# The first weight block on ScalarE's queue, and the first weight sums behind a product's outputs on VectorE

## The chip, the cores and the metric

The kernel runs on one core of a Trainium2 chip. The metric is the device time of one execution in microseconds (us), given as the median of several executions. "Span" is the time from the first to the last instruction of a profiled or recorded execution; it is some 1.8 us shorter than the time. Engines: PE is TensorE's matmul, PEld its weight load, DVE VectorE, ACT ScalarE, POOL GpSimd, SP SyncE. A name like L392 is line 392 of the kernel that ran; from the loads on, lines of the changed kernel are up to three lower than those of the kernel before.

## The reference, cut to what matters

```python
x = A_x
h = x + _A_ref(_layernorm(x), A_wqkv, A_wo)                      # local attention, 32 heads
h2 = h + _B_ref(_layernorm(h), B_w_gate, B_w_up, B_w_down)       # (gate * up) @ down
# x: 2048 x 1024 bf16; wqkv: 1024 x 3072; w_gate, w_up: 1024 x 3584; w_down: 3584 x 1024
```

The 2048 rows are processed in four chunks of 512. The last two chunks share their feed-forward stage, in 14 "pairs" of weight columns that use a Strassen-like scheme with seven products in place of eight; it needs sums of weight blocks (tile sw) and sums of activation blocks (tile prodx).

## The kernel before

Two places matter. The first is the head: the first row tiles, the first weight block, and the LayerNorm that the first matmuls wait for.

```python
    def load_x0(t):                        # one row tile, 128 x 1024: 262 KB
        nc.sync.dma_start(x0[t][:], x[bass.ds(t * 128, 128), :])
    def load_w0(lo, n):                    # half of the first weight block: 524 KB
        nc.sync.dma_start(w0[:, lo:lo + n, :], wqkv_v[:, lo:lo + n, 0:512])
    load_x0(0); load_x0(1); load_w0(0, 4); load_x0(2); load_w0(4, 4); load_x0(3)   # six lines in the kernel
    nc.scalar.preload_act_table_set("natural_log_exp_and_others")
    # ...
    first_half(0, 0); first_half(0, 1); first_rstd(0)   # statistics of row tile 0
    for t in range(4):
        if t < 3:
            first_half(t + 1, 0)           # half the statistics of the next tile, ahead of
        first_norm(t)                      # the normalization of this one
        # ... matmuls of tile t - 1 (first_mm), transposes of tile t on PE
```

The second is the joint between the down projection of chunk 1 and the first pair. `dprod` is 14 matmuls into an accumulator, `result` reads the accumulator on VectorE and stores rows.

```python
    def weight_sums(n, eng=nc.gpsimd):
        # ...
        if n == 0:
            nc.scalar.activation(wt[:], raw[:], ACTF.Copy, scale=scale_gu.s)   # tile ws, one op of 3.7 us
        # ...  four tensor_tensor on eng into sw
    # ...
    for t in range(4):
        ln_rows(3, t, l3)                  # ScalarE normalizes, then a DMA transposes into l3
    sub([dn["kx"], dn["vx"]], dn["21"], dn["11"])
    weight_sums(0, nc.vector)
    retire(2)
    # ...
    for q in range(2):
        dprod(ex[q], q, EF["21"], fcells(dn["12"]), False)
        nc.vector.tensor_tensor(et[:], p5t[:, q, :], hs1[2 + q][:, 512:1024], ALU.add)
        result(1, hs1[2 + q], 2 + q, 1, ex[q], dn["inv"], et)
    retire(1)
    activation_sums(l2, l3, dn["px"])      # four tensor_tensor on VectorE, read l2 and l3
    for q in range(2):
        dprod(ey[q], q, EF["12"], fcells(dn["22"]), False)
        nc.vector.tensor_tensor(p5t[:, q, :], p5t[:, q, :], hs1[q][:, 512:1024], ALU.add)
        result(1, hs1[q], q, 1, ey[q], dn["inv"], p5t[:, q, :])
    for q in range(2):
        dprod(ex[q], q, EF["22"], fcells([dn["kx"], dn["vx"]]), False)   # ex again
        result(1, hs1[2 + q], 2 + q, 0, ex[q], dn["inv"], None)
    # ... then pair 0, 1, ... 13
```

Of the kernel before, what the change touches and what calls it, by code (L numbers as in the profile page):

```python
# [78 lines left out]
def kernel(  # L79
# [11 lines left out]
    nc = tc.nc  # L91
# [18 lines left out]
    wqkv_v = A_wqkv.rearrange("(ko p) n -> p ko n", p=128)  # L110
# [62 lines left out]
    def retire(n=1):  # L173
        state["live"] -= n
        pump()
# [91 lines left out]
    w0 = wpool.tile([128, KO, 512], BF, tag="w", name="w_qkv_0")  # L267
# [4 lines left out]
    def load_x0(t):  # L272
        nc.sync.dma_start(x0[t][:], x[bass.ds(t * 128, 128), :])

    def load_w0(lo, n):
        nc.sync.dma_start(w0[:, lo:lo + n, :], wqkv_v[:, lo:lo + n, 0:512])

    load_x0(0)
    load_x0(1)
    load_w0(0, 4)  # L280
    load_x0(2)
    load_w0(4, 4)
    load_x0(3)
    nc.scalar.preload_act_table_set("natural_log_exp_and_others")
    warm = t1k.tile([128, TC], BF, tag="t1k", name="warm")
    nc.vector.memset(warm[:], 0.0)
# [363 lines left out]
    def weight_sums(n, eng=nc.gpsimd):  # L650
        raw = pair["w", n]
        wt = wpool.tile([128, KO, 2, 256], F16, tag="w", name=f"ws_{n}")
        if n == 0:
            nc.scalar.activation(wt[:], raw[:], ACTF.Copy, scale=scale_gu.s)
        else:
            nc.vector.tensor_scalar(wt[:], raw[:], scale_gu.s, None, ALU.mult)
        sw = wpool.tile([128, 2, 4, 4, 128], F16, tag="w", name=f"sw_{n}")
        for i in ((slice(0, 2),) if eng is nc.vector else (slice(0, 1), slice(1, 2))):
            a11, a21, a12, a22 = (wt[:, k:k + 4, i, c:c + 128].rearrange("p k i c -> p i k c")
                                  for k in (0, 4) for c in (0, 128))  # L660
            eng.tensor_tensor(sw[:, i, 0], a21, a22, ALU.add)  # L661
            eng.tensor_tensor(sw[:, i, 1], sw[:, i, 0], a11, ALU.subtract)
            eng.tensor_tensor(sw[:, i, 2], a11, a21, ALU.subtract)
            eng.tensor_tensor(sw[:, i, 3], a12, sw[:, i, 1], ALU.subtract)
        pair["a", n], pair["s", n] = wt, sw
        state["live"] += 1

    def activation_sums(l2, l3, room):
        b11, b12, b21, b22 = l2[:, 0:4, :], l3[:, 0:4, :], l2[:, 4:8, :], l3[:, 4:8, :]

        t1, t2, t3, t4 = (room[:, bass.ts(i, 4), :].bitcast(F16) for i in range(4))
        nc.vector.tensor_tensor(t1, b12, b11, ALU.subtract)
        nc.vector.tensor_tensor(t2, b22, t1, ALU.subtract)
        nc.vector.tensor_tensor(t3, b22, b12, ALU.subtract)
        nc.vector.tensor_tensor(t4, b21, t2, ALU.subtract)
        pair["b"] = (b11, b21, t1, t2, t3, t4, b22)
# [101 lines left out]
    def sub(dst, x0, x1, eng=nc.vector):  # L778
        for d, a0, a1 in zip(dst, x0, x1):
            eng.tensor_tensor(f16(d[:, 0:NH, :]), f16(a0[:, 0:NH, :]), f16(a1[:, 0:NH, :]), ALU.subtract)  # L780

    def fcells(homes):
        return [f16(t[:, k, :]) for t in homes for k in range(NH)]

    def dprod(ps, q, lhs, rhs, fresh, lo=0, n=TC):
        for k in range(NP):
            nc.tensor.matmul(ps[:, bass.ds(lo, n)], lhsT=lhs[k][:, bass.ts(q, 128)], rhs=rhs[k][:, bass.ds(lo, n)],  # L787
                             start=(fresh and k == 0), stop=(k == NP - 1), skip_group_check=not fresh)

    def result(c, rows, t, hf, ps, sc, other, lo=0, n=TC):  # L790
        cols = bass.ds(hf * 512 + lo, n)
        nc.vector.scalar_tensor_tensor(rows[:, cols], ps[:, bass.ds(lo, n)], sc,
                                       rows[:, cols] if other is None else other[:, bass.ds(lo, n)], ALU.mult, ALU.add)
        nc.sync.dma_start(outf[bass.ds(c * TC + t * 128, 128), cols], rows[:, cols])
# [175 lines left out]
    for t in range(4):  # L970
        ln_rows(3, t, l3)
    sub([dn["kx"], dn["vx"]], dn["21"], dn["11"])
    weight_sums(0, nc.vector)
    retire(2)
    et = att.tile([128, TC], F32, tag="t3", name="et")
    for q in range(2):
# [2 lines left out]
        result(1, hs1[2 + q], 2 + q, 1, ex[q], dn["inv"], et)  # L979
    retire(1)  # L980
    activation_sums(l2, l3, dn["px"])
    for q in range(2):
        dprod(ey[q], q, EF["12"], fcells(dn["22"]), False)
        nc.vector.tensor_tensor(p5t[:, q, :], p5t[:, q, :], hs1[q][:, 512:1024], ALU.add)
        result(1, hs1[q], q, 1, ey[q], dn["inv"], p5t[:, q, :])
# [140 lines left out]
```

## Time and profile before

| | kernel before |
|---|---|
| median time, 3 runs | 783.46 us (782.1 to 784.1) |
| the profiled execution | 781.72 us, span 779.9 us |
| PE busy | 766.8 us, 98% of the span |
| mean granted PE clock, profiled execution | 0.999 |
| largest wait of PE | 3.18 us, for the read of ex |

### The profile page before, as it was taken

The numbers are of one execution on the slowest core, as the hardware profiler recorded it, in microseconds if no ns is written. First come the engines' busy times: TensorE is split into PE (matmuls) and PEld (weight loads), VectorE is DVE, ScalarE is ACT, GpSimd is POOL, SyncE is SP. The second block draws the span as 40 slices with busy tenths as digits, with TensorE's granted clock in tenths as the row PEclk, the third lists the DMA queues.
The fourth block names the chain that finished last, engine by engine and source line by source line (L and its number), as shares of the span: only waits on it lengthen the run. The fifth ranks groups of instructions, "written<-read, shape, count | busy, mean of one in ns | idle before, by whom it ended". The sixth has DMA issues, their size and how long they took to land.

```text
span 779.9 us, 10436 instructions
## 1 busy us (share of the span) xinstructions
PE 766.8 (98%) x3648; PEld 355.0 (46%) x3707; DVE 614.9 (79%) x805; ACT 473.5 (61%) x1028; POOL 142.4 (18%) x152
## 2 busy tenths in 40 slices
PE   8999999999999999999999999989999999999997
PEld 6544444444444444444444444434444444444444
DVE  6629999999899998999979989975553444579862
ACT  5627445313576652966769799836677677788240
POOL 0000000010000200002000001008778677600000
PEclk9999999999999999999999999999999999999999
DMA  8999693896955868858555492824332323730001
GB/s 272 260 236 209 169 274 90 262 274 173 341 174 186 297 215 234 270 189 270 195 163 195 133 313 75 183 74 110 106 99 64 108 67 97 255 123 28 1 27 55
DMA packets 181605, 133.86 MB, mean 172 GB/s; under 512 B 79024, under 2 KB 174384, under 8 KB 179504
## 3 DMA queue, kind: packets, MB, share of 16 engines
q1 hardware_dynamic: 177968, 111.17, 50.1%
q0 software_dynamic: 3584, 22.02, 8.1%
q8 instruction: 29, 0.48, 0.3%
q14 instruction: 24, 0.20, 0.1%
HBM read 104.86 MB, written 22.02 MB: 163 GB/s over the span
## 4 chain that ended last, share of the span: by engine, by line
PE 88%; DVE 9%; ACT 1%; issue 1%; DMA 1%; SPq 0%; DVEq 0%
PE ps L392 20%; PE pu L392 12%; PE pg L392 12%; PE dx L787 6%; PE pz L680 6%; PE acc L626 6%; PE py L680 6%; PE px L680 6%; PE wo L513 4%; PE pv L680 3%; PE dy L787 3%; DVE h L834 1%; PE ps L355 1%; PE ex L787 1%; DVE prodx L780 1%
## 5 line engine op out<-in xcount | busy, mean ns | idle before, releaser
L392 PE MATMUL ps<-lnT,w_qkv 128*128 128x512 bf16 x721 | 158.9, 379 | 0.8
L392 PEld LDWEIGHTS <-w_qkv 128*128 128x128 bf16 x736 | 71.9, 98 | 85.9
L392 PE MATMUL pu<-lnT,w_wu 128*128 128x512 bf16 x438 | 105.1, 379 | 0.6
L392 PE MATMUL pg<-lnT,w_wg 128*128 128x512 bf16 x440 | 105.1, 379 | 0.4
L306 ACT CAST sg<-ps 128x512 bf16<-128x512 f32 x96 | 54.8, 590 | 54.4 <-PE ps L392 51.1
L475 DVE TENSOR_TENSOR pv<-vD,at 128x4096 bf16<-128x4096 bf16 x32 | 72.5, 2287 | 0.3
L432 DVE TENSOR_TENSOR prod<-qD,kD 128x4096 bf16<-128x4096 bf16 x32 | 72.3, 2284 | 0.1
L680 PEld LDWEIGHTS <-sw 128*128 128x128 f16 x448 | 43.8, 98 | 53.2 <-issue 0.4
L392 PEld LDWEIGHTS <-w_wg 128*128 128x128 bf16 x448 | 43.8, 98 | 52.9
L392 PEld LDWEIGHTS <-w_wu 128*128 128x128 bf16 x448 | 43.8, 98 | 52.9
L596 ACT CAST us<-pu 128x512 bf16<-128x512 f32 x56 | 33.2, 593 | 41.1 <-PE pu L392 38.7
L680 PE MATMUL px<-lnT,ws 128*128 128x512 bf16 x212 | 53.1, 379 | 0.6
L680 PEld LDWEIGHTS <-ws 128*128 128x128 f16 x336 | 32.9, 98 | 39.6
L626 PE MATMUL acc<-w_wd,gs 128*128 128x512 bf16 x219 | 48.2, 379 | 0.3
L487 POOL DMA_DIRECT2D od<-oD x4 | 2.2, 544 | 252.3 <-DVE oD L485 162.5
L661 POOL TENSOR_TENSOR sw<-ws 128x512 f16<-128x512 f16 x26 | 30.0, 1154 | 87.6 <-PE py L680 80.4
L591 ACT CAST gs<-pg 128x512 bf16<-128x512 f32 x56 | 32.9, 587 | 11.4 <-PE pg L392 9.3
L185 ACT ACTIVATE rs<-mv,eps 128x1 f32<-128x1 f32 (+1 forms) x25 | 7.4, 297 | 50.3 <-DVE mv L182 47.1
L434 DVE TENSOR_TENSOR prod<-prod 128x4096 bf16<-128x4096 bf16 x16 | 36.6, 2288 | 0.3
L541 ACT ACTIVATE junkd<-w_wd 128x512 bf16<-128x512 bf16 x56 | 34.3, 613 | 0.0
L626 PEld LDWEIGHTS <-gs 128*128 128x128 bf16 x224 | 21.9, 98 | 26.4
L697 ACT COPY py<-px 128x512 f32<-128x512 f32 x28 | 16.0, 570 | 29.6 <-PE px L680 29.6
(304 smaller groups left out, 1398.0 us busy)
## 6 DMA issues: line engine op xcount, KB each, us to landing
w_wg<-in_B_w_gate_dram SPq DMA_DIRECT2D x14, 1024.0 KB, 6.6
w_wu<-in_B_w_up_dram SPq DMA_DIRECT2D x14, 1024.0 KB, 5.3
w_wd<-in_B_w_down_dram SPq DMA_DIRECT2D x8, 896.0 KB, 7.4
w_pair<-in_B_w_gate_dram SPq DMA_DIRECT2D x14, 512.0 KB, 4.0
w_pair<-in_B_w_up_dram SPq DMA_DIRECT2D x14, 512.0 KB, 5.2
w_wo<-in_A_wo_dram SPq DMA_DIRECT2D x6, 1024.0 KB, 8.4
w_qkv<-in_A_wqkv_dram SPq DMA_DIRECT2D x5, 1024.0 KB, 9.1
kd<-sg SPq DMA_DIRECT2D x32, 144.0 KB, 2.9
```

The costliest lines, as they stand in the source:

```text
L306: nc.scalar.copy(sg[:, HB:HB + TC], ps[:])
L392: nc.tensor.matmul(ps[:], lhsT=wt[:, ko, bass.ts(j, 128)], rhs=rhs[:, ko, :], start=(ko == 0), stop=(ko == KO - 1))
L432: nc.vector.tensor_tensor(prod[:, j], qD[:], kD[:, :, o:o + SUB], ALU.mult)
L434: nc.vector.tensor_tensor(prod[:, :, 0:16], prod[:, :, 0:16], prod[:, :, 16:32], ALU.add)
L475: nc.vector.tensor_tensor(pv[:, j], vD[:, :, o:o + SUB], at[:, w, None, :].to_broadcast((128, DH, SUB)), ALU.mult)
L513: nc.tensor.matmul(ps[:], lhsT=oTs[c][:, kk, t, :], rhs=wts["wo", c, hf][:, kk, :], start=(kk == 0), stop=(kk == KO - 1))
L541: nc.scalar.activation(junk, src, ACTF.Abs, accum_out=self.l1[:, k:k + 1])
L591: nc.scalar.copy(gs[:], pg[:])
L596: nc.scalar.copy(us[:], pu[:])
L626: nc.tensor.matmul(acc[t][:], lhsT=hT[f][:, bass.ts(t, 128)], rhs=wts["wd", c, hf, b][:, j, :], start=(f == 0), stop=(f == NF - 1))
L680: nc.tensor.matmul(ps[:], lhsT=lhs[:, ko, :], rhs=rhs[:, ko, :], start=(fresh and ko == 0), stop=(ko == 3), skip_group_check=not fresh)
L787: nc.tensor.matmul(ps[:, bass.ds(lo, n)], lhsT=lhs[k][:, bass.ts(q, 128)], rhs=rhs[k][:, bass.ds(lo, n)], start=(fresh and k == 0), stop=( ...
```

## The change

The intent of its first part (A) is that the weights don't queue between the row tiles: ScalarE issues the two weight halves while SyncE issues the rows. The intent of its second part (B) is that VectorE reads the accumulators of a finished product before it waits for ScalarE's conversion and makes weight sums, so that PE can go on.

```diff
     def load_w0(lo, n):
-        nc.sync.dma_start(w0[:, lo:lo + n, :], wqkv_v[:, lo:lo + n, 0:512])
-
-    load_x0(0)
-    load_x0(1)
+        nc.scalar.dma_start(w0[:, lo:lo + n, :], wqkv_v[:, lo:lo + n, 0:512])
+
     load_w0(0, 4)
-    load_x0(2)
     load_w0(4, 4)
-    load_x0(3)
+    for t in range(4):
+        load_x0(t)
     nc.scalar.preload_act_table_set("natural_log_exp_and_others")
@@
     sub([dn["kx"], dn["vx"]], dn["21"], dn["11"])
-    weight_sums(0, nc.vector)
     retire(2)
@@
     activation_sums(l2, l3, dn["px"])
+    weight_sums(0, nc.vector)
     for q in range(2):
```

## The prediction

> **What bounds the kernel now.** I read the page first. TensorE (PE) is busy for nearly the whole span, and the table of waits of PE alone then shows what is left of its idle time:
>
> ```profile
> span 779.9 us, 10436 instructions
> PE 766.8 (98%) x3648; PEld 355.0 (46%) x3707; DVE 614.9 (79%) x805; ACT 473.5 (61%) x1028; POOL 142.4 (18%) x152
> ```
>
> ```profile
> PE ex L787 <- DVE h L792: 3.2, 1, 3.2
> PE warm_ps L300 <- DVE warm L286: 1.2, 1, 1.2
> ...
> PE ps L355 <- DMA w_qkv<-in_A_wqkv_dram: 0.2, 1, 0.2
> PE pv L680 <- DVE h L792: 0.2, 1, 0.2
> ```
>
> The columns are waiter, what it waited for, us in total, count, longest. The largest single wait is one of 3.2 us by a matmul into the accumulator ex, for VectorE's line 792, which reads the finished sums out of ex. The diff touches exactly this place, and the place of the 0.2 us wait for w_qkv. The timeline around the first (start, duration, engine, instruction, idle time before it) gives the order:
>
> ```profile
> 503.96 2.02 DVE L780 TENSOR_TENSOR vx<-w_dn,w_dn 128x3584 f16<-128x3584 f16 x1
> ...
> 506.69 3.69 ACT L654 ACTIVATE ws<-w_pair,sbgu 128x4096 f16<-128x4096 bf16 x1
> ...
> 510.42 0.69 DVE L661 TENSOR_TENSOR sw<-ws 128x1024 f16<-128x1024 f16 x1 [4.44 <-ACT ws L654]
> ...
> 513.75 0.75 DVE L792 SCALAR_TENSOR_TENSOR h<-ex,inv_h1d,et 128x512 bf16<-128x512 f32 x1
> ...
> 514.56 1.67 PE L787 MATMUL ex<-kx,gs 128*128 128x512 f16 x7 [3.18 <-DVE h L792]
> ...
> 516.00 1.22 DVE L672 TENSOR_TENSOR prodx<-lnT,lnT 128x2048 f16<-128x2048 bf16 x1
> ...
> 520.67 0.68 DVE L984 TENSOR_TENSOR ep<-ep,h 128x512 f32<-128x512 f32 x1
> ...
> 524.37 1.02 PE L680 MATMUL pv<-prodx,sw 128*128 128x512 f16 x4 [0.16 <-DVE h L792]
> ```
>
> VectorE stands still for 4.44 us for ScalarE's conversion ws, then makes the weight sums sw, and only then reads ex, which PE had finished at about 505.2. Behind it come the four activation sums (L672 to L675) and four results. From 460 to 524 the chain that ended last runs mostly over VectorE; from 524 to the last stage it runs over PE without a gap. So time taken from this spot should come off the end one for one.
>
> Last, the start of the timeline:
>
> ```profile
> 3.54 1.29 DVE L330 BATCH_NORM_STATS2 st<-x 128x6 f32<-128x512 bf16 x2 [2.38 <-DMA x<-in_A_x_dram]
> ...
> 5.67 0.73 DVE L342 TENSOR_SCALAR ln<-x,mv,rs 128x512 bf16<-128x512 bf16 x2
> ...
> 8.50 0.62 PE L355 MATMUL ps<-lnT,w_qkv 128*128 128x128 bf16 x8 [0.24 <-DMA w_qkv<-in_A_wqkv_dram]
> 8.76 0.69 DVE L330 BATCH_NORM_STATS2 st<-x 128x6 f32<-128x512 bf16 x1
> ```
>
> The first row tile is there at 3.54 and starts the LayerNorm; the second half of the first weight block is there at 8.5, and PE lost only 0.24 us on it.
>
> [...]an issue takes 0.40 to 0.51 us on SyncE, while between 4 and 8 us the DMA engines are fully busy (shares 1.08, 1.02, 0.99, 1.05 in the windows of 1 us). [...]The activation sums took 1216 to 1226 ns, [...]and moving them doesn't change their cost. [...]L792 ran at 513.75, though its input had long been ready.
>
> **Part B, the weight sums behind the results.** No instruction is added or removed; the order on VectorE changes. ScalarE has no work between ws and the copies of the pair, so ws still runs at 506.69 to 510.4.
> - Two adds and two results (L978, L792) took from 512.96 to about 516.0, that is 3.0 us. They can follow vx, which ends at 505.98, so they end at about 509. PE finishes its product into ey at about 511.4 and goes on to ex at once: the 3.18 us wait is gone.
> - The activation sums need the last transposed LayerNorm rows. The last of the eight transposes (L870) was issued at 507.7, and these take 3.2 to 3.3 us to land: about 511.0. The DMA engines agree: share 1.09 at 509 to 510, 0.26 at 510 to 511, 0 after. VectorE thus still waits, about 2 us, now for a DMA: from 509 to 511.05.
> - Then four activation sums, 516.00 to 520.67 before: 4.67 us, to 515.7. Then four weight sums, 510.42 to 512.96 before: 2.54 us, to 518.3. ws is long ready.
> - L984 and the results thus start at 518.3 instead of 520.67: 2.4 us earlier. PE ends ex at 511.4 + 6.04 (28 matmuls) = 517.4 and the two px products at 519.15. Then its first pv needs the bank of ey: it was read at 522.2 before, now at 519.8 (PE waits 0.65 us). The second pv needs that of ex: 524.37 before, now about 521.95 (PE waits about 0.4 us).
> So part B gives **2.4 us**, not 3.2: VectorE's chain is the bound in the end, and its new start is the landing of the transposes. GpSimd's sums for pair 1 and later loads move along.
>
> **Part A, the first loads.** It removes nothing from the 2.10 MB to be loaded: four row tiles of 262 KB, two half weight blocks of 524 KB. Rates in the windows from 1 us on: 27, 289, 275, 366, 357, 313, 385, 86 GB/s. Added up (316 KB at 3 us, 591 at 4, 957 at 5, 1314 at 6, 1627 at 7, 2012 at 8), in the order of before the bytes of row tile 0 are through at 2.8, tile 1 at 3.8, weight half 1 at 5.3, tile 2 at 6.0, weight half 2 at 7.5. Tile 0 is used at 3.54 and weight half 2 at 8.5, so the landing adds some 0.75 to 0.95 us. SyncE issues tile 0 at 0.76 already; ScalarE's two issues take an estimated 0.9 us ahead of its table load of 1.28 us, which ends at about 3, before its first work at 5.10: harmless. What changes is who shares the DMA engines:
> - **Equal bytes for both queues:** tile 0 is through when 524 KB are, at 3.8, so used at about 4.5; tile 1 at 5.3, used at 6.05, and VectorE reads half of it before it normalizes tile 0. Normalization moves from 5.67 to about 6.7; weight half 2 comes last, at about 9. The second tile's transposes start at about 9.7 instead of 8.9: **+0.8 us**.
> [...]
> - **A rate without the dips** (370 GB/s from 1.9 us on): all landed at 8.4, tile 0 at 4.1: **+0.35 us**.
> From 8.5 on PE is busy without a break, so a later start moves everything. I take **+0.55 us**.
>
> **Sum:** 783.46 - 2.4 + 0.55 = 781.6.
>
> **Rivals.** (1) *The head gets faster*: if the rows keep their time and both weight halves come earlier, the 0.24 us wait goes and the head gains 0.2: 780.9. For it: the issues of all rows end at 2.6 instead of 3.7. Against: the DMA engines are full from 4 to 8 us. (2) *The new wait eats part B*: if the transposes land later, or the weight sums turn out to hold PE at the first pv for longer, B gives 1 us or less: 783. For it: eight transposes queued for 13.4 us. Against: the DMA engines run dry at 510.3. (3) *The whole 3.3 us come off* (both waits of PE): 780.7. Against: VectorE's chain counted above. (4) *The head suffers more*, over 1.5 us, if weights go ahead of rows: 782.6.
>
> **Range and chances.** All these lie between 780.7 and 783. The three timed runs of before spread from 782.1 to 784.1, so a median may be off by some 0.8 us. That makes 779.9 to 783.3. 2% are 15.7 us; no rival comes near, so same 0.98, and 0.01 on each side.
>
> **What would show it.** Right: no 3.2 us wait of PE for L792; VectorE waiting about 2 us for the transposes ahead of L672; weight sums directly behind L675; two waits of PE of half a us ahead of pv; first normalization later than 5.67, at 6 to 6.7. Wrong: L672 starting well before or after 511; normalization at 5.67 or earlier; a second 3 us wait in the pair stage; or the last stage, from the pairs' end to the end of the span, taking other than its 89.6 us.

The sum is 783.46 - 2.4 + 0.55 = 781.6. Its 0.55 us for part A was my choice among cases of how two queues share the DMA engines, and one of them (+0.6 us) is cut: it took over a rule of sharing that no run here shows. The two that stand, +0.8 and +0.35 us, rest on an assumption, equal bytes for both queues; only their rates and landing times are worked out from the profile of the kernel before.

## The result, and the profile after

| | before | after |
|---|---|---|
| median time, 4 runs each | 783.59 us (782.1 to 784.1) | 780.18 us (779.73 to 780.64) |
| span of the profiled execution | 779.9 us | 778.0 us |
| PE busy in it | 98% | 99% |

The ratio is 0.996, 95% interval 0.9942 to 0.9977. Ratios here are the mean time of one kernel's fast runs over that of the other's of the same rounds, so not quite the ratio of the medians. The verdict at 2% is "same", the time is inside the predicted range. But the medians differ by 3.4 us, and the two profiled executions by 2.0 us (781.72 and 779.73). The prediction of 1.85 us matches the profiles, not the medians.

The waits of PE in the changed kernel (waiter, waited for, us in total, count, longest):

```profile
PE warm_ps L298 <- DVE warm L284: 1.2, 1, 1.2
PE pv L678 <- DVE h L790: 0.9, 2, 0.7
...
PE ps L353 <- ACT lnT L348: 0.4, 1, 0.4
```

The 3.2 us wait is gone; two short ones ahead of pv stand in its place, and the wait for w_qkv is gone too. The timeline of the changed kernel at the joint:

```profile
508.73 0.75 DVE L790 SCALAR_TENSOR_TENSOR h<-ex,inv_h1d,et 128x512 bf16<-128x512 f32 x1
...
511.48 1.22 DVE L670 TENSOR_TENSOR prodx<-lnT,lnT 128x2048 f16<-128x2048 bf16 x1 [2.00 <-DMA out_dram<-h]
511.66 1.67 PE L785 MATMUL ex<-kx,gs 128*128 128x512 f16 x7
...
516.15 0.68 DVE L659 TENSOR_TENSOR sw<-ws 128x1024 f16<-128x1024 f16 x1
...
518.68 0.68 DVE L982 TENSOR_TENSOR ep<-ep,h 128x512 f32<-128x512 f32 x1
...
520.27 1.02 PE L678 MATMUL pv<-prodx,sw 128*128 128x512 f16 x4 [0.68 <-DVE h L790]
...
522.38 1.02 PE L678 MATMUL pv<-prodx,sw 128*128 128x512 f16 x4 [0.23 <-DVE h L790]
```

VectorE reads ex before it makes sw, PE goes from ey to ex without a wait at 511.66, and VectorE waits 2.00 us for a DMA ahead of the first activation sum. (The trace names the store of h as that DMA; a run below shows that it is the transposed rows.) The second pv starts at 522.38 instead of 524.37.

The head of the changed kernel, from its timeline:

```profile
3.76 1.29 DVE L328 BATCH_NORM_STATS2 st<-x 128x6 f32<-128x512 bf16 x2 [2.60 <-DMA x<-in_A_x_dram]
...
5.89 0.69 DVE L328 BATCH_NORM_STATS2 st<-x 128x6 f32<-128x512 bf16 x1 [0.60 <-DMA x<-in_A_x_dram]
6.50 0.72 DVE L340 TENSOR_SCALAR ln<-x,mv,rs 128x512 bf16<-128x512 bf16 x2
...
17.12 3.19 PE L390 MATMUL ps<-lnT,w_qkv 128*128 128x512 bf16 x14
```

VectorE waits 0.60 us for row tile 1, and normalizes tile 0 at 6.50 instead of 5.67. The first matmul of 512 columns, which ends the head, starts at 17.12; in the first profile of the kernel before it started at 16.68:

```profile
16.68 2.54 PE L392 MATMUL ps<-lnT,w_qkv 128*128 128x512 bf16 x10
```

So in these two profiles the head loses 0.44 us and the joint gains 2.43 us (524.37 - 522.38 + 0.44): together 1.99 us, the difference of the two executions. What is left to explain is the other 1.4 us of the medians.

### The profile page after: what moved, and what is told of

It is laid out like the page before. It is cut to its first block, busy times and chain, and to the rows that moved or that the text cites. A ratio compares the mean times of both kernels' runs of the same rounds, so it can differ in the third digit from the quotient of the medians.

```text
span 778.0 us, 10494 instructions
## 1 busy us (share of the span) xinstructions
PE 770.7 (99%) x3707; PEld 355.2 (46%) x3707; DVE 614.8 (79%) x805; ACT 473.3 (61%) x1028; POOL 142.1 (18%) x152
## 4 chain that ended last, share of the span: by engine, by line
PE 89%; DVE 9%; DMA 1%; issue 0%; ACT 0%; SPq 0%; DVEq 0%
PE ps L390 20%; PE pu L390 12%; PE pg L390 12%; PE dx L785 6%; PE pz L678 6%; PE acc L624 6%; PE py L678 6%; PE px L678 6%; PE wo L511 4%; PE pv L678 3%; PE dy L785 3%; DVE h L832 1%; PE ps L353 1%; PE ex L785 1%; DVE h L790 1%; DVE prodx L778 1%
## 5 line engine op out<-in xcount | busy, mean ns | idle before, releaser
L678 PE MATMUL px<-lnT,ws 128*128 128x512 bf16 x224 | 55.2, 379 | 0.0
```

The lines of the kernel that those rows point to most:

```text
L678: nc.tensor.matmul(ps[:], lhsT=lhs[:, ko, :], rhs=rhs[:, ko, :], start=(fresh and ko == 0), stop=(ko == 3), skip_group_check=not fresh)
```

## The experiments

All kernels gave correct results. "Before" means the kernel before, run on the same chip in the same rounds.

**Part A alone, and part B alone.** For A alone, `weight_sums(0, nc.vector)` goes back ahead of `retire(2)`; for B alone, the loads go back to SyncE:

```diff
-    load_w0(0, 4)               # nc.scalar.dma_start
-    load_w0(4, 4)
-    for t in range(4):
-        load_x0(t)
+    load_x0(0); load_x0(1); load_w0(0, 4); load_x0(2); load_w0(4, 4); load_x0(3)   # nc.sync.dma_start
```

> Part A alone (first weight block from ScalarE's queue, weight sums where they were). Theory 1, read from the two profiles: the head ends 0.45 us later (the first big matmul at about 17.1 instead of 16.7) and nothing else moves, so the time is 0.4 to 0.5 us above the kernel before and the 3.2 us wait of PE for line 792's read of ex stays. Theory 2, read from the medians (783.59 to 780.18, 1.5 us more than the profiles' 1.9): part A itself makes the kernel faster in most runs, because the kernel before often loses more in its head than in its profiled run; then this run is 1 us or more below the kernel before.

> Part B alone (weight sums behind the activation sums, the loads as before). Theory 1: 2.4 us below the kernel before, 0.45 us below the full change; VectorE waits about 2 us ahead of the first activation sum, PE has no 3 us wait, and the second pv of pair 0 starts at about 521.9. Theory 2: only some 1.9 us below the kernel before, and above the full change by 1 us or more.

Measured, five runs each: A alone 783.64 us (781.99 to 785.29), ratio to before 0.999 (0.9976 to 1.0004); B alone 780.19 us (779.61 to 780.29), ratio 0.995 (0.9937 to 0.9962); before, nine runs, 783.81 us (783.03 to 785.07). Part A by itself is not to be told from nothing: the interval runs from 1.9 us below to 0.3 us above. That leaves no room for the 0.4 to 0.5 us of theory 1, and does not exclude theory 2 by itself; the last pair of runs below does. Part B by itself gives 3.6 us, more than the 2.4 us of the order on VectorE, so neither theory of the second expectation has the size. B alone and the full change (780.18 us) have the same median. They were run at other times.

The profile of A alone fell on an execution of 785.29 us and shows what I had not thought of. Its windows of 1 us around the old wait (busy us of each engine, then the granted PE clock, DMA share, GB/s):

```profile
512.00:513.00 1.00, 0.17 (x1) 0.00 (x0) 0.97 (x3) 0.00 (x0) 0.00 (x0) 1.00 0.00 0
513.00:514.00 1.00, 0.00 (x0) 0.00 (x0) 1.00 (x2) 0.00 (x0) 0.00 (x0) 1.00 0.00 0
514.00:515.00 1.00, 0.00 (x0) 0.00 (x0) 0.89 (x3) 0.00 (x0) 0.00 (x0) 0.75 0.00 0
515.00:516.00 1.00, 0.29 (x1) 0.11 (x1) 0.97 (x2) 0.00 (x0) 0.00 (x0) 0.50 0.00 0
...
520.00:521.00 1.00, 1.00 (x4) 0.37 (x3) 1.00 (x2) 0.00 (x0) 0.00 (x0) 0.50 0.00 0
521.00:522.00 1.00, 1.00 (x5) 0.42 (x4) 1.00 (x2) 0.00 (x0) 0.00 (x0) 0.84 0.06 16
```

While PE waits for the read of ex, its granted clock falls to one half (0.75 in the slice from 514 on, then 0.50), and it is back only at 521.3 (0.84 in the slice from 521 on). What the slices lack of full clock adds up to 6.8 us at one half. Its matmuls of that stretch show it (timeline of PE, A alone):

```profile
515.71 3.15 PE L785 MATMUL ex<-kx,gs 128*128 128x512 f16 x7 [3.54 <-DVE h L790]
...
523.00 1.67 PE L785 MATMUL ex<-vx,gs 128*128 128x512 f16 x7
```

Seven matmuls took 3.15 us where seven took 1.67 us later. The wait of PE thus had a second price in this execution beside its own length. The mean clock of each execution is recorded for timed runs too. Over a span of 780 us, half the clock for 6.8 us takes 0.004 off it, and for 3.4 us (a drop of this length is in a profile below) 0.002; a 0.999 without that comes from the last microseconds of the kernel (1.07 us at half clock in the first profile of before). The kernel before had 0.996 to 0.998 in eight of nine runs and 0.999 in one (783.03 us, its fastest). A alone had 0.996 to 0.997 in four runs, and 1.0 in the one of 781.99 us. B alone had 1.0 in all five. The first profile of the kernel before, with its full clock at the wait, had been a lucky draw.

**ScalarE's loads behind its table load.** The full change with one line moved:

```diff
+    nc.scalar.preload_act_table_set("natural_log_exp_and_others")
     load_w0(0, 4)
     load_w0(4, 4)
     # ...
-    nc.scalar.preload_act_table_set("natural_log_exp_and_others")
```

> The full change, but ScalarE's two loads stand behind its table load of 1.28 us. [...]Theory: [...]with the weights issued 1.3 us later, row tiles 0 and 1 pass first, statistics start at 3.5 or earlier and don't wait for tile 1, so the head is 0.4 us faster than in the full change. Rival: the cost is the sharing of the DMA engines by two queues as such; then tile 1 is still late (statistics of it wait until 5.5 or later) and the time equals that of the full change.

Measured: 779.93 us (779.59 to 780.2), the full change's time; clock 0.999 or 1.0 in all runs. But the edit did not do what it was for. From the timeline of this run:

```profile
0.75 1.28 ACT L278 ACT_TABLE_LOAD   x1 [0.75 <-PEq L1108]
...
0.78 1.01 ACTq L276 DMA_DIRECT2D w_qkv<-in_A_wqkv_dram  x2
```

ScalarE's sequencer issued both loads from 0.78 on while the table load ran (0.75 to 2.03), so the weights were not issued later. The run says nothing on its two theories. The profile of the full change shows more of the head: which DMA queue moved how much in stretches of half a microsecond (queue, packets, MB, share of the 16 engines; q1 carries SyncE's rows, q10 ScalarE's weights). The stretches shown are 3.5 to 4, 4.5 to 5 and 5 to 5.5 us:

```profile
q10 hardware_dynamic: 187, 0.19, 107.5%
...
q1 hardware_dynamic: 97, 0.19, 96.7%
q10 hardware_dynamic: 18, 0.01, 8.5%
...
q10 hardware_dynamic: 157, 0.16, 92.0%
q1 hardware_dynamic: 22, 0.02, 14.2%
```

In this profile the two queues' shares were far from even: 107.5% of the engines for the weights and none for the rows in the first of these stretches, 8.5% and 96.7% in the second, 92.0% and 14.2% in the third. Added up over all stretches, q1 moved 0.26 MB until 3.5 us, the size of a row tile (262 KB); q10 had moved 0.52 MB by 4.5 us, the size of a weight half (524 KB); and q1 moved its next 0.26 MB between 4 and 5.5 us. Between 6 and 6.5 us both moved (119 weight and 31 row packets). So row tile 1 came behind as many bytes as the first weight half has, and VectorE waited 0.60 us for it, until 5.89.

**A version with VectorE's new wait filled.** On top of part B alone, the add and the result of ey 0 and the second add go ahead of the activation sums:

```diff
-    activation_sums(l2, l3, dn["px"])
-    weight_sums(0, nc.vector)
     for q in range(2):
         dprod(ey[q], q, EF["12"], fcells(dn["22"]), False)
         nc.vector.tensor_tensor(p5t[:, q, :], p5t[:, q, :], hs1[q][:, 512:1024], ALU.add)
-        result(1, hs1[q], q, 1, ey[q], dn["inv"], p5t[:, q, :])
+        if q == 0:
+            result(1, hs1[0], 0, 1, ey[0], dn["inv"], p5t[:, 0, :])
+    activation_sums(l2, l3, dn["px"])
+    weight_sums(0, nc.vector)
+    result(1, hs1[1], 1, 1, ey[1], dn["inv"], p5t[:, 1, :])
```

> Part B alone with the two adds into ep and the result of ey 0 put ahead of the activation sums, into VectorE's 2 us wait for the transposes. Theory: that wait is real idle time and VectorE's chain behind it is the bound; 2.1 us of work go into it, PE has no wait ahead of either pv, and the time is 1.2 us below part B alone (3.6 us below the kernel before). Rival: the wait ends with something that the work before it delays (the store of the results rather than the transposes); then the activation sums start later than 511.1 and the gain is under 0.5 us.

Measured: 778.60 us (778.56 to 778.98), ratio to before 0.9932 (0.992 to 0.9945); 1.6 us below part B alone. From its timeline:

```profile
510.92 0.68 DVE L982 TENSOR_TENSOR ep<-ep,h 128x512 f32<-128x512 f32 x1
511.52 1.22 DVE L672 TENSOR_TENSOR prodx<-lnT,lnT 128x2048 f16<-128x2048 bf16 x1
...
521.24 1.03 PE L680 MATMUL pv<-prodx,sw 128*128 128x512 f16 x4
```

The activation sums start where they did (511.39 in part B alone, whose head ended 0.12 us earlier), with no wait ahead of them, and the second pv starts at 521.24 without a wait. In part B alone it started at 522.30. That is 1.2 us when the 0.12 us of the head is taken off, as expected; the medians show 0.4 us more, which I can't assign. The new wait was real idle time and VectorE's chain behind it was the bound.

**PE's old wait filled with useless matmuls.** The kernel before, with 12 matmuls added, so that VectorE's order and the position of ex's read stay as they are:

```diff
+    fill = psum.tile([128, TC], F32, tag="mm", name="fill")
+    for k in range(12):
+        nc.tensor.matmul(fill[:], lhsT=EF["12"][k][:, 0:128], rhs=fcells(dn["22"])[k], start=(k == 0), stop=(k == 11))
     for q in range(2):
         dprod(ex[q], q, EF["22"], fcells([dn["kx"], dn["vx"]]), False)
```

> The kernel before, unchanged in order, with 12 more matmuls into a spare bank (operands of the product ey, nothing reads them) in PE's 3.2 us wait. VectorE's chain is as long as before, so a fast-clock run can't be shorter. Theory, from part A alone, whose profile shows PE's granted clock at one half for 6.8 us right after this wait: in most runs of the kernel before the wait also lowers PE's clock; with the wait filled the clock is 0.999 or 1.0 in every run and the time falls to about 782.0, that is 1.4 to 2.1 us below the kernel before (its one profiled run with the full clock: 781.7). Rival: the clock has no share in it (the part of the gain beyond 2.4 us comes from the head or from noise); then the time equals the kernel before's within 0.5 us.

Measured: 782.65 us (782.2 to 783.42), before 783.54 us (782.55 to 785.03, nine runs); ratio 0.999 (0.9977 to 1.0003). The clock is 1.0 in all five runs, against 0.997 or 0.998 in seven of nine of before. So the kernel did more work on PE and lost no clock. The gain is 0.9 us of the expected 1.4 to 2.1, and its interval touches no change, so in time alone this is not clear; the clock readings are. (In the profiled execution, 783.29 us, VectorE also waited 0.78 us for ScalarE at 488, ahead of the added matmuls; the first profile of before has no such wait.) The timed runs of before agree with it: the three with a mean clock of 0.999 or 1.0 average 782.9 us, the fifteen others 784.1 us. The five filled runs average 782.8 us. The step from here to part B alone, 782.65 to 780.19 us, is 2.46 us: this is the order on VectorE without the clock (across two calls).

**What the activation sums wait for.** Part B alone, the stores of the two results of ex held back:

```diff
-        result(1, hs1[2 + q], 2 + q, 1, ex[q], dn["inv"], et)
+        nc.vector.scalar_tensor_tensor(hs1[2 + q][:, 512:1024], ex[q][:], dn["inv"], et[:], ALU.mult, ALU.add)
     retire(1)
     activation_sums(l2, l3, dn["px"])
+    for q in range(2):
+        nc.vector.tensor_copy(hs1[2 + q][:, 512:513], hs1[2 + q][:, 512:513])
+        nc.sync.dma_start(outf[bass.ds(TC + (2 + q) * 128, 128), 512:1024], hs1[2 + q][:, 512:1024])
```

> Part B alone, with the stores of the two results of ex not issued until the activation sums are done (a one-column copy onto itself after them makes the stores wait). The trace puts VectorE's 2 us wait ahead of the first activation sum down to the store of h. Theory: it is the transposed rows; the first activation sum starts at 511.0 to 511.6 as in part B alone (511.39). Rival: it is the store that the sum waits for; then the sum starts right behind the result, at about 509.5.

```profile
510.96 1.22 DVE L672 TENSOR_TENSOR prodx<-lnT,lnT 128x2048 f16<-128x2048 bf16 x1 [2.05 <-DMA lnT<-lnr]
```

The stores were issued at 515.8, and the sum still waited 2.05 us, now put down to the transposes. (510.96 is a little under the expected stretch because the head ended early here, 16.55 against 17.09.) Time 779.46 us over two runs. The store is out.

**Part A once more, without the clock's noise.** The filled version was repeated, and run with part A's loads (the diff of the change's first half on top of it):

> The hoisted version of part B once more, as the partner of the next run. All theories: 778.6 as before, clock 1.0.

> The hoisted version with part A's loads. No run of these two has a clock drop, so part A is seen without that noise. Theory 1, from the profile of the full change against that of the kernel before: 0.45 us slower than the run ahead of it. Theory 2, from the heads of all profiles taken since (first big matmul at 16.7, 17.1, 17.2 with the loads on one queue; 17.1, 17.5, 17.5 with two): some 0.3 us slower. Theory 3: no difference, under 0.15 us.

Measured, five runs each: 778.70 us (778.63 to 779.34) with the loads on one queue, 778.61 us (778.4 to 778.62) with two. Theories 1 and 2 fall. Theory 3 holds for the medians, which differ by 0.09 us; but all five runs with two queues lie below all five with one, and the means differ by 0.29 us. So part A is worth 0 to 0.3 us here, in its favour. With two queues the runs spread 0.2 us, with one 0.7 us. This last version has a median of 778.61 us, within 0.01 us of the lowest here, a ratio to before of 0.9935 (0.9923 to 0.9948), and beats both the kernel before and the changed one.

**The kernel before, three more profiles.**

> The kernel before, unchanged, for a second profile. Its first profile was one of the few executions with PE's clock at full speed all through. Theory (the clock drop belongs to PE's 3 us wait): this profile most likely shows PE's granted clock at one half in a stretch that begins within 3 us of the start of that wait and lasts one or two times 3.4 us, matmuls of that stretch start some 0.43 us apart instead of 0.215, and the mean clock is 0.996 to 0.998. Rival: drops fall anywhere in the kernel; then this one, if there is any, lies elsewhere.

> The kernel before once more, for the rule behind the drop. Part A alone dropped with PE busy 25% of the 3.41 us window in which its wait began[...]; the two profiles of before, with 50% and 47% in their emptier window, did not. [...]Rival: drops are unrelated to the grid[...].

> The same again, for another position of the wait on the grid: a drop of 3.4 or 6.8 us[...].

(The last two expected a rule for when the clock falls, on a grid of such windows. These runs don't show it. The shares are measured, in stretches of 3.41 us whose place was my choice: in A alone PE was busy for 0.84 us of 511.33 to 514.74, in the first profile of before for 1.71 us of 512.86 to 516.27, in the second for 1.61 us of 513.90 to 517.31.)

The second profile (782.84 us) had no drop at the wait: its clock is 1.00 in all windows of 3 us from 505 to 526, and its mean of 0.999 leaves no room for one of 3.4 us elsewhere, which would take 0.002 off it. My guess that it most likely would have a drop was a miss. The third (783.63 us, 0.998) and the fourth (783.91 us, 0.997) had lower clocks at the old wait. From the windows of the third:

```profile
515.00:516.00 1.00, 0.92 (x5) 0.45 (x5) 0.86 (x3) 0.00 (x0) 0.00 (x0) 1.00 0.06 20
516.00:517.00 1.00, 1.00 (x5) 0.36 (x4) 1.00 (x2) 0.00 (x0) 0.00 (x0) 0.61 0.33 111
...
519.00:520.00 1.00, 1.00 (x5) 0.40 (x4) 1.00 (x1) 0.00 (x0) 0.00 (x0) 0.68 0.06 16
```

What the slices from 516 to 520 lack of full clock (the two left out show 0.50) adds up to 3.4 us at one half, from 516.2 on. For the fourth the matmuls show it: from the end of the wait, seven took 3.14 us, the next seven 1.77 and the seven after these 1.67. All runs beside each other:

| run | wait of PE for ex | PE's clock at the wait and after it |
|---|---|---|
| before, 1st profile | 3.18 us, to 514.56 | 1.00 in every us from 511 to 519 |
| before, 2nd | 3.19 us, to 515.70 | 1.00 in all windows from 505 to 526 |
| before, 3rd | 3.18 us, to 515.08 | one half for 3.4 us from 516.2 |
| before, 4th | 3.19 us, to 515.55 | seven matmuls in 3.14 us; mean clock of the run 0.997 |
| A alone | 3.54 us, to 515.71 | one half for 6.8 us from 514.5 |
| before with filled wait | 1.46 us, to 516.17 | seven matmuls in 1.67 us; mean clock of the run 1.0 |
| the full change | none | 1.00 in all windows from 508 to 524 |

So the clock was lower at the wait or after it in three of these five executions with a wait of over 3 us, and not in two, whose waits of 3.18 and 3.19 us were as long as those of two of the three. What decides between them is left open here. This is one reason why executions of one and the same kernel differ; the head, which ended anywhere from 16.68 to 17.82, is another.

## Why the prediction was right or wrong

The range held the time, and the reading of the joint held almost to the digit. But the sum was short, 1.85 us for 3.4 us. All cases in the prediction's list lie between 780.7 and 783, and the measured 780.18 is below them all: only the 0.8 us added for noise took it in, which is luck. (That 0.8 us on top of 783 would give 783.8 as the upper end, not 783.3.)

**Part B, step by step.** In the changed kernel's profile, with the 0.44 us of its later head taken off, VectorE's results of ex end at 509.0 (predicted about 509), the activation sums start at 511.04 (511.05), L982 starts at 518.24 (518.3), and the second pv at 521.94 (521.95). PE's two waits ahead of pv are 0.68 and 0.23 us (0.65 and 0.4). The new bound, the landing of the transposed rows, was named rightly, and shown by holding back the stores. The 2.4 us are there: 2.43 in the profiles, 2.46 between medians where the clock plays no part. The last stage, from the first matmul into dx, takes 89.8 us in both profiles, so what was gained at the joint came off the end.

**Part A.** A head longer by 0.55 us was predicted, and the pair of profiles has 0.44. Normalization came at 6.50 (6 to 6.7 predicted). The way there differed: the bytes were not shared evenly (8.5% of the engines for the weights and 96.7% for the rows between 4.5 and 5 us); row tile 0 was used at 3.76, not at 4.1 to 4.5, the weights were in time, and what delays is row tile 1. The step that failed is the base line. The head of the first profile of before was among its best: its first large matmul started at 16.68, in the other three profiles of the same kernel at 17.82, 17.16 and 17.66, and in the experiments with one queue at 16.55 to 17.42. With two queues it started at 17.12 to 17.47. On average the two orders are about equal (17.2 over nine profiles with one queue, 17.3 over four with two), and the medians of the last pair of runs differ by only 0.09 us. The 0.24 us wait of PE for the second weight half, which the prediction took as typical, was lucky too. The longest wait of PE for w_qkv in the third profile of before, and the one for VectorE's normalized rows in the last version, with two queues:

```profile
PE ps L355 <- DMA w_qkv<-in_A_wqkv_dram: 0.7, 1, 0.7
...
PE pt L347 <- DVE ln L340: 1.0, 1, 1.0
```

With one queue, PE waited 0.6 to 1.0 us for w_qkv in six of nine profiles. With two it never did, but waited 0.5 to 1.2 us for the rows (0.6 us or less, or no wait listed, with one). Part A trades one wait for the other. SyncE's last row issue ended at 2.7 us instead of 3.7, and the median of the last pair changed by 0.09 us (778.70 to 778.61).

**The term that was missing.** The prediction counted PE's wait only by its length and what stands behind it. The step "all these lie between 780.7 and 783", and with it the whole list of rivals, left out that PE's clock can be lower after its wait, 0.50 in A alone and in the third profile of before. The mean clock was 0.999 in the one execution whose profile I had. Part B removes the wait, and with it the drop (1.0 in all five runs of B alone). Its size: with a drop of 3.4 us, the second pv started 11.17 us after PE's wait ended (third profile: 515.08 to 526.25) instead of 9.81 (514.56 to 524.37), so 1.4 us (1.2 us in the fourth profile); with one of 6.8 us (A alone, 515.71 to 527.96) 2.4 us.

The spans add up. Take the first profile's 779.9 us, add what the head lost against 16.68 and what the clock cost. The third profile: 779.9 + 0.48 + 1.36 = 781.7, measured 781.8. The second, without a drop: 779.9 + 1.14 = 781.0, measured 781.1. The fourth: 779.9 + 0.98 + 1.21 = 782.1, measured 782.1. A alone, whose wait was 0.36 us longer: 779.9 + 0.79 + 0.36 + 2.44 = 783.5, measured 783.5. The changed kernel: 779.9 + 0.44 - 2.43 = 777.9, measured 778.0. So of the 3.4 us between the medians, about 2.4 are the order on VectorE. The remaining 1.0 us is put down to the clock, to the accuracy of these runs: 0.9 us by filling the wait, whose interval includes zero, and 1.2 us between the runs of before with and without a lowered clock. That the drop goes with the wait is shown by filling it; its share of the medians is a remainder. Part A is 0.3 us at most.

**The rivals.** Rival 3 (the whole 3.3 us off, 780.7) has about the right time by a wrong way: VectorE's chain did bound, as the two waits ahead of pv show, and the hoisted version could still take 1.2 us from it. Rival 4 (a much slower head) is excluded by the last pair of part A; rival 1 (a head faster by 0.2 us) is not, since that pair allows 0 to 0.3 us; rival 2 (the new wait eats the gain) is excluded by the 2.00 us wait that lay where it was counted.

## What to carry to other kernels

Price a wait of TensorE like this one by more than its length: after waits of 3.2 to 3.5 us the clock was at one half for 3.4 us in one profile and for 6.8 us in another, and in two profiles of the kernel before it stayed at 1.00. One profile may thus miss it, so compare the clocks of the timed runs before trusting one. When the order of work on an engine is changed, count on to the next thing it waits for; here a wait of 2.00 us for transposes took the place, and moving ready work into it gave 1.6 us more. A second DMA queue sped up a start whose DMA engines were already full (shares of 0.99 to 1.08 from 4 to 8 us in the first profile of before) by 0.3 us at most.
